# Holding the first token block's instructions to their written order, with the list scheduler ordering the rest

## The chip, the core and the metric

The kernel runs on one core of a Trainium2 chip. The metric is the device time of one execution in microseconds; the time before is 1110.92 us, the median of three runs (1110.46 to 1111.63). A core has five engines that each work through a queue of their own in order: TensorE (PE in the profile, with its weight loads as PEld), VectorE (DVE), ScalarE (ACT), GpSimd (POOL) and SyncE (SP), which issues nearly all DMAs here. They wait for one another through semaphores.

## The reference

An attention layer with two kinds of keys is followed by a mixture of four experts.

```python
k_sum = k.reshape(B, H, nb, block, D).max(axis=3)      # B, H, S, D = 4, 8, 768, 64
v_sum = v.reshape(B, H, nb, block, D).mean(axis=3)     # block 32, so 24 blocks
scores_l = scale * q @ k.T                             # kept only where |i - j| < 16
scores_s = scale * q @ k_sum.T + log(block)
a = softmax(concat([scores_l, scores_s]))
x = (a @ concat([v, v_sum])).reshape(B * S, H * D)     # 3072 tokens x 512
p = domain_probs / domain_probs.sum(-1)
for e in range(4):                                     # w1[e] 512 x 1024, w2[e] 1024 x 512
    out += p[:, e] * (relu(x @ w1[e]) @ w2[e])
```

## The kernel before

Tokens are worked on in eight blocks of 384 (`TB`), two to each batch entry. The attention of a block is cut into eight pieces: four query groups of 96 queries (`QB`) by two groups of four heads (`G`). Piece n is query group n // 2 and head group n % 2; a piece sees a window of 128 keys and the 24 block summaries.

**The first block** (`first_tokens`) is written apart from the rest. Its eight pieces run in the order 0, 2, 4, 6, 1, 3, 5, 7. Every piece has 18 steps: scores in two halves (tile `psc`, 64-row matmuls in f32), maxima and subtraction on DVE (`ms`, `nb`), exponentials on ACT, a summary copy (`sm`), transposes (`pT`), copies out of PSUM (ACT for `pT`, DVE for `sT`), the product with the values (`pav`, called the gather), the division on DVE (`rs`, `xt`), two transposes of the quotient (again into `pav`, called the x turn) and the two parts of the result (`xh` on ACT, `xl` on DVE). Beside the pieces stand block maxima of k (`ksr`, DVE), block means of v by matmul (`pvf`, from `vn`), and, for expert 0, four early halves of the first product (`ph` 0 to 3, the half whose inputs come from head group 0). The table `STEPS` gives each step an offset, `T0` the distance of pieces, `KEYS` the places of the other work; the steps are sorted by these numbers, so the calls are made in an interleaved order that was set by hand.

**All later work** is written in a loop: `plan` names the blocks and experts, and `advance` puts the attention pieces of the next blocks (pieces 8, 9, ... with `stage_a`, `scores`, `probs`, `transposed`, `values`, `to_x`) between the units of the matmuls `ph` (x by w1) and `po` (h by w2). Weights are loaded in raw form (`wr`, four buffers) and split into a high part by ACT and a rest by POOL (w1) or DVE (w2 while one block is worked on). A transposing DMA turns a piece's weights `aw` into `awT`, from which PE makes `px`.

**What sets the order.** No call issues anything: a call appends a `Step` to the list `program`. At the end `order_of(program, bufs_of)` reads the operands, finds which step must follow which (data, and the buffers of each tile tag), and lets a list scheduler with its own costs pick the sequence: each engine takes, among the steps whose inputs are there, the one with the lowest rank, which is PE's nominal time of the work that needs it. The result is issued in that sequence, and that is the order of each engine's queue. So the order in which the first block's calls were made is only one input of the ranks; an engine may take any other ready step first.

`in_order` and `early` do not exist before the change. `Step.behind` maps the number of a step that must come first to a flag: with True the scheduler waits for its end and a semaphore, with False only for its start.

Of the kernel before, what the change touches and what calls it, by code (L numbers as in the profile page):

```python
# [64 lines left out]
WAIT = dict(PE=53, ACT=33, DVE=33, POOL=76, SP=28)  # L65
# [7 lines left out]
@cache  # L73
def footprint(offset, pairs, wide):

    (step, parts), *rest = pairs
    mask = (1 << wide) - 1
    for s, n in reversed(rest):
        if s and n > 1:
            one, mask = mask, 0  # L80
            for k in range(n):
                mask |= one << (s * wide * k)
    return offset // step, offset // step + parts, mask << (offset % step * wide)
# [75 lines left out]
        return 400.0, ((1350.0 if store else 1950.0) + SPARE_DMA, t * 1.2)  # L159


def order_of(steps, bufs):

    used, live = {}, {}
    for n, s in enumerate(steps):
        seen = {}
        for ap, w in [(x, True) for x in s.written] + [(x, False) for x in s.read]:
            name, tag = ap.tensor.name, getattr(ap.tensor, "tag", None)  # L170
            if tag is None:
                continue
            p0, p1, mask = footprint(ap.offset, ap.ap, BYTES[ap.dtype] // 2)
            kept = []
            for at in live.get(name, ()):
                m, a0, a1, was, wrote = at
                if m != n and (w or wrote) and a0 < p1 and p0 < a1:
                    chain = s.key == "PE" == steps[m].key
                    if was & mask or chain:
                        full = not chain and (wrote or steps[m].key != s.key)  # L180
                        s.behind[m] = max(s.behind.get(m, False), full)
                        if w and not was & ~mask and a0 >= p0 and a1 <= p1:
                            continue
                kept.append(at)
            live[name] = [*kept, (n, p0, p1, mask, w)]
            seen[name] = tag
        for name, tag in seen.items():
            used.setdefault(tag, {}).setdefault(name, []).append(n)
        s.tiles = list(seen.items())
        for m, full in s.behind.items():  # L190
            steps[m].ahead.append((n, full))
    queue = {tag: sorted(tiles, key=lambda t: tiles[t][0]) for tag, tiles in used.items()}


    nominal, now = {}, 0.0
    for n, s in enumerate(steps):
        if s.key == "PE":
            nominal[n] = now
            now += s.takes
    freed = {}  # L200
    for tag, names in queue.items():
        for old, new in zip(names, names[bufs[tag] :]):
            first = used[tag][new][0]
            for m in used[tag][old]:
                if m < first:
                    freed.setdefault(m, []).append(first)
    due, place = {}, now
    for n in range(len(steps) - 1, -1, -1):
        s = steps[n]
        place = nominal.get(n, place)  # L210
        end = sum(s.lasts) if s.key == "SP" else s.lasts
        d = [due[m] - (end + WAIT[steps[m].key] if full else s.takes) for m, full in s.ahead]
        d += [due[m] - end - WAIT[steps[m].key] for m in freed.get(n, ())]
        due[n] = min(nominal.get(n, math.inf), *d) if d else nominal.get(n, math.inf)
        if due[n] == math.inf:
            due[n] = place + 30000.0
    rank = [nominal.get(n, due[n]) for n in range(len(steps))]


    left = [len(s.behind) + len(s.tiles) for s in steps]  # L220
    ready = [0.0] * len(steps)
    uses = {name: len(at) for tiles in used.values() for name, at in tiles.items()}
    gone, given = {}, {}
    coming = {k: [] for k in WAIT}
    waiting = {k: [] for k in WAIT}
    free = dict.fromkeys(WAIT, 0.0)
    lanes, wire, order = [0.0] * LANES, 0.0, []

    def loosen(n, t):
        ready[n] = max(ready[n], t)  # L230
        left[n] -= 1
        if not left[n]:
            heapq.heappush(coming[steps[n].key], (ready[n], n))

    def give(tag, t):
        k = given[tag] = given.get(tag, -1) + 1
        if k < len(queue[tag]):
            for n in used[tag][queue[tag][k]]:
                loosen(n, t + WAIT[steps[n].key] if t else 0.0)

    for n, s in enumerate(steps):
        if not left[n]:
            heapq.heappush(coming[s.key], (0.0, n))
    for tag in queue:
        for _ in range(bufs[tag]):
            give(tag, 0.0)
    while len(order) < len(steps):
        best = None
        for k in WAIT:
            t = max(free[k], lanes[0] + WAIT[k]) if k == "SP" else free[k]  # L250
            while coming[k] and coming[k][0][0] <= t:
                n = heapq.heappop(coming[k])[1]
                heapq.heappush(waiting[k], (rank[n], n))
            if not waiting[k]:
                if not coming[k]:
                    continue
                t = coming[k][0][0]
            if best is None or t < best[0]:
                best = t, k
        t, k = best  # L260
        while coming[k] and coming[k][0][0] <= t:
            n = heapq.heappop(coming[k])[1]
            heapq.heappush(waiting[k], (rank[n], n))
        n = heapq.heappop(waiting[k])[1]
        s = steps[n]
        order.append(n)
        free[k] = t + s.takes
        if k == "SP":
            wire = end = max(wire, t + s.lasts[0]) + s.lasts[1]
            lanes = [*lanes[1:], end]  # L270
        else:
            end = t + s.lasts
        for m, full in s.ahead:
            loosen(m, end + WAIT[steps[m].key] if full else t + 1.0)
        for name, tag in s.tiles:
            uses[name] -= 1
            gone[name] = max(gone.get(name, 0.0), end)
            if not uses[name]:
                give(tag, gone[name])
    return order  # L280
# [3 lines left out]
def attn_moe(ctx: ExitStack, tc: tile.TileContext, qvL, qv0, v0L, kD, kT, vT, w1L, w2L, dpL, cst, out):  # L284
    nc = tc.nc
    program, bufs_of = [], {}

    class Engine:
# [11 lines left out]
    V, A, PL, PE, SP = (  # L300
        Engine(e, k)
        for e, k in ((nc.vector, "DVE"), (nc.scalar, "ACT"), (nc.gpsimd, "POOL"), (nc.tensor, "PE"), (nc.sync, "SP"))
    )
# [97 lines left out]
    def mixing():  # L401
        SP.dma_start(pw, dpL)
        s = const.tile([P, NT, 1], F32, name="dps")
        V.tensor_reduce(s, pw, axis=AX.X, op=ALU.add)
        V.tensor_scalar_add(s, s, EPS)
        V.reciprocal(s, s)
        V.tensor_tensor(pw, pw, s.broadcast_to([P, NT, E]), op=ALU.mult)
# [87 lines left out]
    def split_v(b, v0):  # L495
        b12 = sb.tile([NST, 2, 512], BF16, name=f"b12_{b}", tag="awT", bufs=2)
        b1, b2 = b12[:, 0, :], b12[:, 1, :]
        V.tensor_copy(b1, v0)
        V.tensor_tensor(v0, v0, b1, op=ALU.subtract)
        V.tensor_copy(b2, v0)  # L500
        V.tensor_tensor(v0, v0, b2, op=ALU.subtract)
        V.tensor_scalar_mul(b1, b1, gsel[0])
        V.scalar_tensor_tensor(b2, b2, gsel[1], b1, op0=ALU.mult, op1=ALU.add)
        vs = sb.tile([NST, H, D], BF16, name=f"vs{b}", tag="vs", bufs=2)
        V.scalar_tensor_tensor(
            vs,
            v0.rearrange("p (h d) -> p h d", d=D),
            gsel[2],
            b2.rearrange("p (h d) -> p h d", d=D),
            op0=ALU.mult,  # L510
            op1=ALU.add,
        )
        vsum[b] = vs
# [963 lines left out]
    steps = []  # L1477
# [19 lines left out]
    def advance(to):  # L1497
        nonlocal at
        while at < len(steps) and steps[at][0] < to:
            steps[at][1](steps[at][2])  # L1500
            at += 1

    EARLY = 4
    ahead = plain_units([0], 0, early=EARLY)
    first_tokens(ahead)
    mixing()
    advance(per)
    split_v(0, *vmean0)
    V.tensor_tensor(high_rows[:NST], gsel[0], gsel[1], op=ALU.add)


    plan = [([0], (0, 1)), ([1], (1, 0)), ([0, 1], (2, 3)), *PAIRS]
    pos = per
    for (tbs, experts), end in zip(plan, ENDS):
        pair = tbs if isinstance(tbs, int) else None
        n = 2 if pair else len(tbs)
# [25 lines left out]
            part()  # L1542
        pos = end

    for n in order_of(program, bufs_of):
        tc.keep_in_program_order(program[n].issue())


# [59 lines left out]
```

## Time and profile before

| what | value |
|---|---|
| median of three runs | 1110.92 us (1110.46 to 1111.63) |
| profiled execution | 1109.61 us |
| its span | 1107.8 us |
| granted PE clock, mean | 0.979 |
| PE busy | 1093.2 us (99%) |
| DVE, ACT, POOL busy | 806.9, 695.1, 563.8 us |

The profiled execution took 1.31 us less than the median. Its span runs from the first to the last recorded instruction; 1.81 us lie outside it. Line 296 is the line at which the helper `Engine` calls the engine, so every group of the profile stands on that one line, and tiles tell the groups apart. The granted clock is the share of full speed that PE's clock had; "busy" on PE counts a matmul that runs at half clock for its whole doubled length.

### The profile page before, as it was taken

The numbers are of one execution on the slowest core, as the hardware profiler recorded it, in microseconds if no ns is written. First come the engines' busy times: TensorE is split into PE (matmuls) and PEld (weight loads), VectorE is DVE, ScalarE is ACT, GpSimd is POOL, SyncE is SP. The second block draws the span as 40 slices with busy tenths as digits, with TensorE's granted clock in tenths as the row PEclk, the third lists the DMA queues.
The fourth block names the chain that finished last, engine by engine and source line by source line (L and its number), as shares of the span: only waits on it lengthen the run. The fifth ranks groups of instructions, "written<-read, shape, count | busy, mean of one in ns | idle before, by whom it ended". The sixth has DMA issues, their size and how long they took to land.

```text
span 1107.8 us, 20496 instructions
## 1 busy us (share of the span) xinstructions
PE 1093.2 (99%) x6994; PEld 760.3 (69%) x6994; DVE 806.9 (73%) x1959; ACT 695.1 (63%) x1882; POOL 563.8 (51%) x650
## 2 busy tenths in 40 slices
PE   8989999999999999999999999999999999999998
PEld 6888888898898765555555565555555468686867
DVE  4479988998988898878776555556545794969473
ACT  3567867775576999887764565556434581838170
POOL 1378976783764989976643313224112251627050
PEclk8589999999999999999999999999999999999999
DMA  7268757777556698787797564474721350514001
GB/s 269 77 202 232 201 159 186 177 201 188 157 165 193 209 307 244 229 250 228 244 296 213 156 171 133 135 229 123 187 83 38 132 160 14 171 47 162 3 15 58
DMA packets 169305, 184.10 MB, mean 166 GB/s; under 512 B 79344, under 2 KB 115184, under 8 KB 169200
## 3 DMA queue, kind: packets, MB, share of 16 engines
q1 hardware_dynamic: 169200, 182.79, 55.7%
q8 instruction: 55, 0.90, 0.3%
q14 instruction: 50, 0.41, 0.1%
HBM read 131.76 MB, written 34.08 MB: 150 GB/s over the span
## 4 chain that ended last, share of the span: by engine, by line
PE 89%; DVE 3%; POOL 2%; DMA 2%; ACT 2%; issue 1%; SPq 0%; POOLq 0%; ACTq 0%; DVEq 0%
PE po L296 30%; PE phb L296 12%; PE ph L296 11%; PE pha L296 8%; PE psc L296 5%; PE pob L296 4%; PE phc L296 4%; PE phd L296 4%; PE poa L296 3%; PE px L296 2%; PE pav L296 2%; PE pod L296 1%; PE poc L296 1%; DMA wr<-in_w1L 1%; PE pT L296 1%
## 5 line engine op out<-in xcount | busy, mean ns | idle before, releaser
L296 PEld LDWEIGHTS <-w1g 128*128 128x128 f16 x2016 | 195.6, 98 | 145.3 <-issue 2.1
L296 PE MATMUL po<-w2s,h 128*128 128x512 f16 x1152 | 279.8, 379 | 0.0
L296 PEld LDWEIGHTS <-h 128*128 128x128 f16 x1584 | 151.7, 98 | 116.4
L296 PE MATMUL phb<-x_t,w1g 128*128 128x384 f16 x864 | 164.1, 326 | 0.8 <-ACT phb L296 0.3
L296 PE MATMUL ph<-xh,w 128*128 128x384 f32 x512 | 141.1, 346 | 0.4 <-ACT xh L296 0.4
L296 POOL TENSOR_TENSOR ks<-kr,ks 128x304 fp32r<-128x304 f32 x112 | 103.3, 926 | 45.5 <-ACT ks L296 38.2
L296 PE MATMUL po<-w,hh 128*128 128x512 f32 x384 | 123.5, 399 | 0.7 <-DVE hl L296 0.7
L296 ACT ACTIVATE ms<-ms,nb 96x152 f32<-96x152 f32 x256 | 104.5, 414 | 18.0 <-DVE nb L296 17.4
L296 DVE CUSTOM_DVE_ANT_0 ms<-psc,c_sb 96x152 f32<-96x152 f32 x256 | 70.9, 306 | 59.9 <-PE psc L296 57.3
L296 PE MATMUL pha<-x,w1g 128*128 128x384 f16 x576 | 111.5, 326 | 0.0
L296 POOL TENSOR_TENSOR w<-wr,w 128x512 fp32r<-128x512 f32 x60 | 84.0, 1408 | 43.9 <-ACT w L296 38.8
L296 POOL TENSOR_TENSOR qs<-qv,qs 64x384 fp32r<-64x384 f32 x56 | 58.7, 1048 | 91.3 <-ACT qs L296 66.3
L296 PEld LDWEIGHTS ph<-xh,w 128*128 128x128 f32 x512 | 94.8, 192 | 1.3 <-ACT xh L296 0.6
L296 PE MATMUL ph<-xl,w 128*128 128x384 f32 x256 | 87.3, 341 | 0.0
L296 POOL TENSOR_TENSOR v<-qv,v 128x256 f16<-128x256 f32 (+1 forms) x56 | 43.0, 768 | 86.3 <-ACT v L296 78.1
L296 PEld LDWEIGHTS po<-w,hh 128*128 128x128 f32 x384 | 69.7, 188 | 16.0 <-DVE hl L296 1.8
L296 POOL TENSOR_TENSOR w2g<-wr,w2g 128x256 f16<-128x256 f32 (+1 forms) x32 | 31.2, 983 | 90.4 <-ACT w2g L296 90.3
L296 PE MATMUL po<-w,hl 128*128 128x512 f32 x192 | 75.8, 395 | 0.0
L296 DVE TENSOR_TENSOR aw<-ms,aw 96x512 f16<-96x512 f32 x112 | 68.5, 639 | 5.5 <-ACT aw L296 4.7
L296 PE MATMUL psc<-ks,qs 128*96 128x152 f32 x448 | 63.8, 265 | 1.7 <-DVE nb L296 0.9
L296 PEld LDWEIGHTS <-hs 128*128 128x128 f16 x576 | 56.3, 98 | 6.6
L296 PEld LDWEIGHTS psc<-ks,qs 128*96 128x96 f32 x448 | 52.7, 164 | 11.5 <-DVE nb L296 1.4
(184 smaller groups left out, 2250.1 us busy)
## 6 DMA issues: line engine op xcount, KB each, us to landing
wr<-in_w2L SPq DMA_DIRECT2D x104, 256.0 KB, 3.1
qv<-in_qvL SPq DMA_DIRECT2D x56, 320.0 KB, 3.3
kr<-in_kD SPq DMA_DIRECT2D x56, 256.0 KB, 3.5
w1g<-wdg SPq DMA_DIRECT2D x28, 512.0 KB, 3.5
wr<-in_w1L SPq DMA_DIRECT2D x44, 256.0 KB, 3.1
w1g<-wdg SPq DMA_DIRECT2D x28, 384.0 KB, 3.1
wx<-in_w1L SPq DMA_DIRECT2D x32, 256.0 KB, 4.2
wdg<-w1g SPq DMA_DIRECT2D x16, 512.0 KB, 4.2
```

What stands on the lines that cost most here:

```text
L296: program.append(Step(self.key, lambda: getattr(self.engine, name)(*a, **kw), name, a, kw))
```

## The change

`order_of` takes a third argument, `early`, with a step number for each engine. A step whose number lies below its engine's entry is put behind the engine's step before it (flag False). `in_order` is filled twice: with the length of the program after `first_tokens` for all five engines, and again after the mixing weights, `advance(per)` (which puts `stage_a` of piece 8), `split_v` and one small sum, for PE, ACT, DVE and POOL. So SP keeps the written order through `first_tokens`, the other four through `split_v`. Steps written later are free, and may still be taken between two held ones. The arithmetic, the tiles, the buffers and the number of instructions of work stay.

```diff
-def order_of(steps, bufs):
+def order_of(steps, bufs, early):
-    used, live = {}, {}
+    used, live, last = {}, {}, {}
     for n, s in enumerate(steps):
...
         s.tiles = list(seen.items())
+        if n < early[s.key]:
+            if s.key in last:
+                s.behind.setdefault(last[s.key], False)
+            last[s.key] = n
         for m, full in s.behind.items():
             steps[m].ahead.append((n, full))
...
     first_tokens(ahead)
+    in_order = dict.fromkeys(WAIT, len(program))
     mixing()
     advance(per)
     split_v(0, *vmean0)
     V.tensor_tensor(high_rows[:NST], gsel[0], gsel[1], op=ALU.add)
+    in_order.update(dict.fromkeys(("PE", "ACT", "DVE", "POOL"), len(program)))
...
-    for n in order_of(program, bufs_of):
+    for n in order_of(program, bufs_of, in_order):
         tc.keep_in_program_order(program[n].issue())
```

In the rows below the first number in a name is the piece (`psc8`), the block (`ph0`) or the layer and expert of a weight (`w10` is w1 of expert 0), and the last one counts tiles. Line 296 of the kernel before is line 300 of the changed one.

**The start, DVE and SP.** DVE behind the maxima of piece 0, before:

```order
L296 COPY vsf0_124<-c_sb_72 96x4
L296 COPY vsf1_173<-c_sb_72 96x4
L296 TENSOR_TENSOR high_rows_73<-c_sb_72 120x1
L296 TENSOR_TENSOR vsf0_124<-pvf0_120,c_sb_72 96x4x64
L296 ISA ms2_126,nb2_127<-psc2_0_122,c_sb_72 96x152
```

and now:

```order
L300 TENSOR_REDUCE ksr0_91<-k02_79 128x24
L300 TENSOR_TENSOR vsf0_124<-pvf0_120,c_sb_72 96x4x64
L300 COPY vsf0_124<-c_sb_72 96x4
L300 ISA ms2_126,nb2_127<-psc2_0_122,c_sb_72 96x152
L300 ISA nb2_127 96x1
```

The block maxima of the third k chunk, which stood behind the first maxima of piece 4, now stand ahead of the value sums and the maxima of piece 2. SP's ninth to thirteenth transfer, before and now:

```order
L296 DMA qv0_2_83<-in_qv0 128x448
L296 DMA qv0_3_84<-in_qv0 128x448
L296 DMA k02_79<-in_kT 128x768
L296 DMA k03_80<-in_kT 128x768
L296 DMA qv0_4_85<-in_qv0 128x448
```

```order
L300 DMA k02_79<-in_kT 128x768
L300 DMA k03_80<-in_kT 128x768
L300 DMA qv0_2_83<-in_qv0 128x448
L300 DMA qv0_3_84<-in_qv0 128x448
L300 DMA wr10_0_103<-in_w1L 128x512
```

The two k chunks went ahead of the queries of the third and fourth piece, and the first two weight tiles ahead of the last four pieces' queries.

**The end of the first block, PE.** Behind the last scores of piece 7, before:

```order
L296 MATMUL ph0_0_0_215<-xh0_0_96,w10_0_140 128x384
L296 MATMUL ph0_0_0_215<-xl0_0_97,w10_0_140 128x384
L296 MATMUL pav1_188<-c_sb_72,xt1_193 128x96 x2
L296 MATMUL pav3_200<-vsf1_173,sT3_196 96x260
L296 MATMUL pav3_200<-vf3_170,pT3_195 96x65 x4
L296 MATMUL ph0_0_0_215<-xh0_0_96,w10_0_140 128x384 x2
L296 MATMUL ph0_0_0_215<-xl0_0_97,w10_0_140 128x384
L296 MATMUL pT5_202<-c_sb_72,ms5_190 128x96 x4
```

and now:

```order
L300 MATMUL pav3_200<-c_sb_72,xt3_206 128x96 x2
L300 MATMUL pav5_211<-vsf1_173,sT5_209 96x260
L300 MATMUL pav5_211<-vf5_185,pT5_208 96x65 x4
L300 MATMUL pT7_212<-c_sb_72,ms7_203 128x96 x4
L300 MATMUL pT7_212<-c_sb_72,sm7_210 96x96
L300 MATMUL ph0_0_0_215<-xh0_0_96,w10_0_140 128x384
L300 MATMUL ph0_0_0_215<-xl0_0_97,w10_0_140 128x384
L300 MATMUL ph0_0_0_215<-xh0_0_96,w10_0_140 128x384 x2
```

The first matmul of the experts came, before, directly behind the scores of piece 7; now two gathers, two sets of transposes and two x turns stand ahead of it that stood behind it.

**The step onto block 1, PE and SP.** PE around the scores of piece 8, before:

```order
L296 MATMUL psc8_0_244<-ks8_0_232,qs8_234 96x152 x4
L296 MATMUL psc8_1_251<-ks8_1_233,qs8_234 96x152 x4
L296 MATMUL pav7_219<-c_sb_72,xt7_222 128x96 x2
L296 MATMUL ph0_0_0_215<-xh0_1_98,w10_0_140 128x384
L296 MATMUL ph0_0_1_220<-xh0_1_98,w10_1_145 128x384
L296 MATMUL ph0_0_2_224<-xh0_1_98,w10_2_176 128x384
L296 MATMUL ph0_0_3_225<-xh0_1_98,w10_3_201 128x384
L296 MATMUL psc9_0_274<-ks9_0_253,qs9_255 96x152 x4
```

and now, 62 `ph` matmuls behind the x turn of piece 7:

```order
L300 MATMUL ph0_0_6_281<-xh0_0_96,w10_6_280 128x384
L300 MATMUL ph0_0_6_281<-xl0_0_97,w10_6_280 128x384
L300 MATMUL psc8_0_244<-ks8_0_232,qs8_234 96x152 x4
L300 MATMUL psc8_1_251<-ks8_1_233,qs8_234 96x152 x4
L300 MATMUL ph0_0_6_281<-xh0_0_96,w10_6_280 128x384 x2
```

The summaries that piece 8 needs come to their place by four small DMAs, `ks0`. On SP before and now:

```order
L296 DMA wr10_3_106<-in_w1L 128x512
L296 DMA qv8_113<-in_qvL 128x640
L296 DMA kr8_112<-in_kD 128x4x128
L296 DMA ks0_230<-ksr0_91 64x4x24 x4
L296 DMA qv9_115<-in_qvL 128x640
```

```order
L300 DMA qv9_115<-in_qvL 128x640
L300 DMA wr10_4_228<-in_w1L 128x512
L300 DMA wr10_5_229<-in_w1L 128x512
L300 DMA ks0_230<-ksr0_91 64x4x24 x4
L300 DMA wr20_4_265<-in_w2L 128x512
```

They went behind two weight tiles, `wr10_4` and `wr10_5`, whose buffers come free only when DVE has split the w2 tiles 0 and 1, and that split now stands behind the division of piece 5 and of piece 7. The queues of before and now are alike again from the second product of block 1 with expert 1 on (PE's last difference stands there).

## The prediction

> **What bounds the kernel now.** First the page: busy time by engine, the clock row (tenths of full speed in forty slices) and two groups with count, busy and mean ns.
>
> ```profile
> PE 1093.2 (99%) x6994; PEld 760.3 (69%) x6994; DVE 806.9 (73%) x1959; ACT 695.1 (63%) x1882; POOL 563.8 (51%) x650
> PEclk8589999999999999999999999999999999999999
> L296 POOL TENSOR_TENSOR ks<-kr,ks 128x304 fp32r<-128x304 f32 x112 | 103.3, 926 | 45.5 <-ACT ks L296 38.2
> L296 POOL TENSOR_TENSOR w<-wr,w 128x512 fp32r<-128x512 f32 x60 | 84.0, 1408 | 43.9 <-ACT w L296 38.8
> ```
>
> PE is never short of work for long: of 1107.8 us only 14.6 are without a matmul. What can be won is therefore idle time of PE and time at a low clock, and both lie in the first 75 us, the stretch that the change orders anew. The busy time by stretch shows the second (us; busy time and instructions of PE, PEld, DVE, ACT, POOL; granted clock; DMA share; GB/s):
>
> ```profile
> 17.60:55.16 37.56, 37.56 (x193) 32.40 (x193) 17.96 (x81) 18.03 (x53) 9.47 (x12) 0.50 0.34 100
> 55.16:65.40 10.24, 7.78 (x59) 6.77 (x58) 7.96 (x26) 7.19 (x21) 9.62 (x9) 1.00 0.51 165
> 65.40:72.22 6.82, 6.04 (x21) 5.53 (x21) 4.91 (x12) 3.33 (x12) 6.24 (x7) 0.50 0.83 270
> 80.00:100.00 20.00, 19.72 (x125) 16.23 (x124) 18.52 (x44) 15.07 (x45) 16.98 (x18) 1.00 0.74 212
> 100.00:120.00 20.00, 20.00 (x155) 18.60 (x154) 18.98 (x45) 16.79 (x49) 15.55 (x17) 1.00 0.90 243
> 120.00:140.00 20.00, 20.00 (x127) 16.64 (x126) 19.15 (x43) 14.40 (x44) 18.48 (x19) 1.00 0.67 189
> 140.00:160.00 20.00, 20.00 (x132) 18.72 (x131) 17.49 (x50) 12.85 (x38) 14.60 (x16) 1.00 0.55 134
> ```
>
> Half clock holds from 17.60 to 55.16, with PE busy all 37.56 us, and from 65.40 to 72.22, with 6.04 busy. Work at half clock takes twice its time, so (37.56 + 6.04) / 2 = 21.8 us are lost. The first stretch is 11, the full-clock one 3 and the second 2 times 3.413 us: the clock changes on a grid. PE's timeline shows the idle time (start, length, operation, in brackets the idle time before it and what ended it):
>
> ```profile
> 9.05 0.30 PE L296 MATMUL pT<-c_sb,ms 96*128 96x96 f32 x1 [1.55 <-ACT ms L296]
> 9.19 2.78 PE L296 MATMUL pvf<-vn,c_sb 128*120 128x256 f32 x12
> 11.90 0.46 PE L296 MATMUL psc<-k,qv 64*96 64x128 f32 x2
> 13.43 0.47 PE L296 MATMUL pT<-c_sb,ms 96*128 96x96 f32 x3
> 13.91 0.46 PE L296 MATMUL psc<-k,qv 64*96 64x128 f32 x2
> 16.78 0.68 PE L296 MATMUL pav<-vsf,sT 96*96 96x260 f32 x2
> 40.48 0.74 PE L296 MATMUL psc<-k,qv 64*96 64x128 f32 x2
> 42.87 1.18 PE L296 MATMUL pav<-vsf,sT 96*96 96x260 f32 x2
> 49.55 0.69 PE L296 MATMUL ph<-xh,w 128*128 128x384 f32 x1
> 64.39 0.38 PE L296 MATMUL pav<-c_sb,xt 96*128 96x96 f32 x2 [2.05 <-DVE xt L296]
> 65.19 1.49 PE L296 MATMUL ph<-xh,w 128*128 128x384 f32 x4 [0.41 <-ACT xh L296]
> 67.47 0.93 PE L296 MATMUL psc<-ks,qs 128*96 128x152 f32 x4 [0.78 <-POOL qs L296]
> ```
>
> From 11.90 to 13.43 and from 13.91 to 16.78 PE did three half-pieces of scores in 4.40 us; at half clock two took 42.87 - 40.48 = 2.39, so three at full clock are some 1.80. The stall on DVE's maxima is 2.6 us there.
>
> **The change, part by part.** *The start.* PE stands idle for 1.55 + 2.6 = 4.15 us before the clock falls. In the new order the first transposes stand behind the value sums, so the first wait becomes one for `vn`. Those sums ran at 9.19 right behind the transposes, so `vn` was in by then; I take 8.75, a wait of 1.25 (bounds 0 and 1.55). The reduce of the third k chunk now stands ahead of the maxima of piece 2 on DVE:
>
> ```profile
> 17.12 0.94 DVE L296 TENSOR_REDUCE ksr<-k 128x24 f32<-128x768 f32 x1
> 10.77 0.40 POOL L296 COPY vf<-qv 128x256 f32<-128x256 f32 x1 [4.30 <-DMA qv<-in_qv]
> 14.52 0.40 POOL L296 COPY vf<-qv 128x256 f32<-128x256 f32 x1 [2.11 <-DMA qv<-in_qv]
> ```
>
> The chunk moves up two places among transfers that came in between 10.77 and 14.52; I estimate 11.8, so DVE is free of it at 12.7, and PE's next scores wait about 0.55. With 0.35 at the first division the idle time is 2.15: **-2.0**. Bounds: all 4.15 gone, or 1 us lost if the chunk comes at 14.5 and holds DVE.
>
> *The half clock.* What ended it? Of the matmuls `ph` alone, three windows of the grid (same columns, PE and PEld first):
>
> ```profile
> 48.33:51.74 3.41, 1.01 (x2) 0.50 (x2) 0.00 (x0) 0.00 (x0) 0.50 0.01 2
> 51.74:55.16 3.42, 1.93 (x5) 1.55 (x6) 0.00 (x0) 0.00 (x0) 0.50 0.37 91
> 65.40:68.81 3.41, 1.90 (x6) 1.52 (x6) 0.00 (x0) 0.00 (x0) 0.50 0.96 323
> 14.19:17.60 3.41, 2.58 (x22) 2.01 (x21) 1.93 (x10) 2.42 (x7) 0.89 (x4) 1.00 1.05 385
> ```
>
> The clock rose behind the second, where PE was full and 1.93 us were `ph`; not behind the first (1.01), and not behind the third, in which PE also stood idle for 0.78. The last row is of all operations, the window behind which it fell, with PE busy for 2.58 of 3.41. So I take it that the rise needs a full window with about 1.9 us of `ph`. [...]
>
> In the new order two gathers, two sets of transposes and two x turns stand ahead of the first `ph` that stood behind it. Their prices at half clock:
>
> ```profile
> 37.34 1.18 PE L296 MATMUL pav<-vsf,sT 96*96 96x260 f32 x2
> 39.54 0.84 PE L296 MATMUL pT<-c_sb,ms 96*128 96x96 f32 x4
> 50.36 0.52 PE L296 MATMUL pav<-c_sb,xt 96*128 96x96 f32 x2
> 50.67 1.07 PE L296 MATMUL pav<-vsf,sT 96*96 96x260 f32 x2
> ```
>
> A gather goes from 37.34 to 39.54 (2.20), a set of transposes to 40.48 (0.94), an x turn 0.31 (0.40 with its start): 2 x 3.54 = 7.08. PE enters the half clock with 2.0 us of full-clock work done ahead, 4.0 us at half clock. The first `ph` comes at 49.55 + 7.08 - 4.0 = 52.6. From there to 55.16 are 2.5 us of `ph`, enough for the clock to rise at 55.16 as before; had it to wait a window, 58.57, 1.7 us dearer, and two, 3.4. The second stretch of half clock followed the idle time around 62 to 66 and goes with it. What is left is 37.56 / 2 = 18.8: **-3.0** (bounds -3.0 and +0.4).
>
> *The idle time at 62 to 68.* 2.05 + 0.41 + 0.78 us. The last division of piece 7 now has the matmuls of `ph` 0 to 6 behind it, and the scores of piece 8, on which PE waited for POOL, stand behind these: **-3.2** (bounds -3.2 and 0, if the wait only moves).
>
> *New waits.* The weights' splits on POOL now decide when `ph` 4 to 7 run. POOL's written string between weight 4 and weight 7 has three `w` at 1.41, four `ks` at 0.93 by the page's means, two `qs` at about 1.0, two `kr` and smaller ones, some 13.5 us together; by my count PE does seven tiles in that time and comes to `ph` 6 half a us early and to `ph` 7 again: **+1.1** (bounds 0 and 3). Sum at PE: -2.0 - 3.0 - 3.2 + 1.1 = **-7.1**.
>
> *The cap.* PE can be that early only if DVE is. From 80 to 160 DVE is busy 18.52 + 18.98 + 19.15 + 17.49 = 74.1 of 80 us, and each `px` needs DVE's `aw`:
>
> ```profile
> 73.92 0.96 DVE L296 TENSOR_TENSOR aw<-ms,aw 96x512 f16<-96x512 f32 x2
> 93.55 0.40 PE L296 MATMUL px<-awT,v 128*64 128x192 f16 x6 [0.28 <-DMA awT<-aw]
> L296 DVE TENSOR_REDUCE vmax<-vch 128x1 f32<-128x768 f32 x4 | 3.8, 941 | 0.0
> L296 DVE TENSOR_REDUCE wmax<-w 128x1 f32<-128x512 f32 x10 | 6.4, 666 | 0.0
> L296 DVE SCALAR_TENSOR_TENSOR hl<-ph,hh 128x384 fp32r<-128x384 f32 x20 | 10.9, 547 | 3.5 <-ACT hh L296 3.3
> L296 DVE SCALAR_TENSOR_TENSOR xs<-px,xs 128x192 f32<-128x192 f32 x8 | 2.7, 343 | 0.9 <-ACT xs L296 0.9
> ```
>
> (The group rows are DVE's between 60 and 160 us.) By my count of the held string, DVE does the `aw` of piece 8 around 79.0 instead of 74.9, with 2.95 us of later work already done: 1.15 behind. But ahead of the `aw` of piece 15 four reductions of `vch`, two `wmax`, one `hl` and one `xs` drop out: 4 x 0.94 + 2 x 0.67 + 0.55 + 0.34 = 6.0. DVE's lead there is 6.0 - 1.15 = 4.8, and about as much where the queues become alike again. So of PE's 7.1 about **5.0** stay: 1109.6 - 5.0 = 1104.6 for an execution like the profiled one. That one lies 1.3 below the median, so the forecast is **1105.9**.
>
> **The rivals.** *One episode, no gain.* PE catches up with the attention at the `px` of piece 8: the `ks0` DMAs, which carry the block summaries, now stand on SP behind two weight tiles that wait for DVE's split of the w2 tiles, so the scores and the `aw` are late. A second stall of the kind at 62 to 68 would cost 3.2 us and two windows of half clock, 3.0: 6.3. -5.0 + 6.3 gives 1112.2; a DVE that gives nothing of the gain on gives 1110.4. For it speaks the small slack at 93.55 (PE waits there for `awT` by 0.28 already); against it that POOL, not `ks0`, ended PE's wait at 67.47.
>
> *Slower: two episodes.* If `ks0` comes so late that pieces 8 and 9 both hold PE, each stall ends in half clock: -5.0 + 12.6 = 1118.5. It decides once `awT` lands 2.4 us or more behind PE's coming to `px`, since a wait of 2.05 and its sequel were what went before the fall at 65.40. Against it: `ph` and `po` of expert 0 lie between, and `ks0` needs only two splits of 0.9 us of DVE's.
>
> *The clock never falls.* [...] As a mechanism here: the fall at 17.60 followed a window of 2.58 busy, and the new order fills that window. It would give 18.8 more at PE, as far as DVE and the transfers let it: 1105.9 - 18.8 = 1087. Against it, at 0.50 full windows did not help; and the rows do not tell what made it fall.
>
> *The hold does nothing* is out: PE's queue differs in a thousand places.
>
> **How the numbers follow.** Within 0.2% (2.2 us) a measurement of this kernel cannot be told from no change. The forecast with its spread (first half clock up to two windows longer, the cap a few us off) has a chance of 0.63, its own range 1102 to 1108.7; the clock that never falls 0.05; one episode or nothing 0.19; two episodes 0.13. The range of 1101.5 to 1111 leaves out the clock's rival, the slower one and the tail of the third. Faster is 0.63 + 0.05 = 0.68, the same 0.19, slower 0.13.
>
> **What would show it.** Right: idle time of PE before 17.6 near 2 us; half clock once, to 55.16; no half clock at 65 to 72; no wait of PE for `xt` of piece 7; waits below 1 us for the POOL tiles of `ph` 6 and 7; DVE some 5 us earlier at 160. Wrong: `px` of piece 8 waiting for `awT` by us and a half clock behind it; a first `ph` behind 53.2, with the clock up at 58.57 or 61.98; or 1.00 in all windows.

## The result and the profile after

The changed kernel takes 1098.70 us (median of four, 1096.94 to 1100.42) against 1110.69 us for the kernel before (median of four): a ratio of 0.9893, 95% interval 0.9874 to 0.9912. That is 12 us less; 5.0 had been forecast, and the time lies below the range. The profiled execution took 1096.94 us with a span of 1095.2. All ratios here leave out executions more than 1.5% above the fastest of the same kernel.

Its page, busy time by engine and the clock in forty slices:

```profile
PE 1077.9 (98%) x6994; PEld 747.4 (68%) x6994; DVE 810.6 (74%) x1959; ACT 694.9 (63%) x1882; POOL 563.9 (51%) x650
PEclk9999999999999999999999999999999999999999
```

The dip of the first two slices, from the half clock between 17.60 and 55.16 us, is gone. PE is busy for 15.3 us less with the same 6994 matmuls, and idle for 17.3 us instead of 14.6. So the span's 12.6 us are 15.3 us of less time at half clock, less 2.7 us of new waits. The windows of the clock's grid, of PE alone (length, PE busy and instructions, granted clock, DMA share, GB/s), before:

```profile
7.36:10.77 3.41, 1.86 (x12) 1.00 1.05 404
10.77:14.19 3.42, 3.01 (x20) 1.00 1.04 399
14.19:17.60 3.41, 2.58 (x22) 1.00 1.05 385
17.60:21.01 3.41, 3.41 (x24) 0.50 1.01 352
```

and after:

```profile
7.85:11.27 3.42, 2.55 (x12) 1.00 1.04 407
11.27:14.68 3.41, 3.41 (x33) 1.00 1.06 394
14.68:18.09 3.41, 3.41 (x34) 1.00 1.04 386
18.09:21.51 3.42, 3.42 (x32) 1.00 1.00 321
52.23:55.64 3.41, 1.95 (x14) 1.00 0.74 225
55.64:59.05 3.41, 3.41 (x14) 0.50 0.32 87
```

The window behind which the clock fell is now full, and the clock stays up through all eight pieces, until PE waits at 53 us. PE's timeline shows its first wait, for the values `vn`; in two gathers one piece apart how long a piece takes at full clock; and in the first `ph` the lead that PE wins (49.55 before):

```profile
8.72 2.82 PE L300 MATMUL pvf<-vn,c_sb 128*120 128x256 f32 x12 [0.98 <-DMA vn<-in_v0L]
18.05 0.68 PE L300 MATMUL pav<-vsf,sT 96*96 96x260 f32 x2
21.81 0.68 PE L300 MATMUL pav<-vsf,sT 96*96 96x260 f32 x2
37.67 0.42 PE L300 MATMUL ph<-xh,w 128*128 128x384 f32 x1
53.16 0.91 PE L300 MATMUL psc<-ks,qs 128*96 128x152 f32 x8 [0.81 <-POOL qs L300]
54.72 0.62 PE L300 MATMUL ph<-xh,w 128*128 128x384 f32 x2 [0.65 <-POOL w L300]
93.87 0.44 PE L300 MATMUL ph<-xh,w 128*128 128x384 f32 x1 [1.31 <-ACT w L300]
151.55 0.92 PE L300 MATMUL psc<-ks,qs 128*96 128x152 f32 x4 [3.30 <-DVE nb L300]
```

A piece takes 21.81 - 18.05 = 3.76 us. PE leads by 11.9 us at the first `ph`. A landmark that exists once, the transpose `pmx` behind the maxima of v (tile view: count, times, first and last start), shows it again later, before and after:

```profile
L296 PE MATMUL pmx<-c_sb,vm x1: 276/276/276, 140.7 to 140.7; 128*1 128x128 f32 x1
L300 PE MATMUL pmx<-c_sb,vm x1: 276/276/276, 124.9 to 124.9; 128*1 128x128 f32 x1
```

The lead is 15.8 us there and 12.6 at the end. The wait of 3.30 us at 151.55 takes most of the difference; half clock follows it (0.91 on the mean from 140 to 160):

```profile
80.00:100.00 20.00, 16.84 (x122) 15.02 (x121) 19.21 (x44) 16.99 (x53) 19.45 (x23) 1.00 0.86 220
140.00:160.00 20.00, 16.70 (x92) 14.38 (x90) 17.94 (x44) 12.94 (x35) 12.80 (x14) 0.91 0.58 172
```

(columns as in the prediction's first windows). From 80 to 100 PE is idle for 3.16 us. Its waits name the splits of the weights, 1.31 and 1.13 us for ACT's part and 0.72 for POOL's. DVE and POOL, busy for 19.21 and 19.45 of 20 us, are likely the bound behind them; no run tests that.

### The profile page after: what moved, and what is told of

Same layout as the page of the kernel before. It is cut to its first block, busy times and chain, and to the rows that moved or that the text cites. A ratio compares the mean times of both kernels' runs of the same rounds, so it can differ in the third digit from the quotient of the medians.

```text
span 1095.2 us, 20517 instructions
## 1 busy us (share of the span) xinstructions
PE 1077.9 (98%) x6994; PEld 747.4 (68%) x6994; DVE 810.6 (74%) x1959; ACT 694.9 (63%) x1882; POOL 563.9 (51%) x650
## 4 chain that ended last, share of the span: by engine, by line
PE 86%; DVE 5%; POOL 3%; ACT 3%; issue 1%; DMA 1%; SPq 0%; POOLq 0%; DVEq 0%; ACTq 0%
PE po L300 30%; PE phb L300 12%; PE ph L300 9%; PE pha L300 8%; PE psc L300 4%; PE pob L300 4%; PE phc L300 4%; PE phd L300 4%; PE poa L300 3%; PE px L300 2%; PE pod L300 1%; PE poc L300 1%; PE pav L300 1%; DVE wmax L300 1%; DVE ms L300 1%
## 5 line engine op out<-in xcount | busy, mean ns | idle before, releaser
L300 DVE TENSOR_TENSOR aw<-ms,aw 96x512 f16<-96x512 f32 x112 | 73.3, 681 | 8.2 <-ACT aw L300 7.8
```

Source lines behind the costliest of these rows:

```text
L300: program.append(Step(self.key, lambda: getattr(self.engine, name)(*a, **kw), name, a, kw))
```

## The experiments

Theory A, formed from these windows: the gain is the clock. Idle time of PE among the small f32 matmuls of the pieces lets it fall, and at half clock these matmuls never raise it again, however full PE is. Theory B: the fall has another cause (the order, the mix of matmuls), or the order brings the gain by itself. Each kernel is compared with the kernel before on the same chip (medians 1109.9 to 1111.5); two changed kernels are compared by their ratios. In experiments 2, 8, 9 and 11 the executions of one kernel lie up to 24 us apart, which is the finding there.

### 1. A stall put back

The changed kernel, with four reduces ahead of the maxima of piece 6.

```diff
...
+    junk = const.tile([P, NB], F32, name="junk")
+    first = min(n for n, s in enumerate(program) if s.written[0].tensor.name.rpartition("_")[0] == "ms6")
     for n in order_of(program, bufs_of, in_order):
+        for _ in range(4 * (n == first)):
+            x = kch0[0].rearrange("p (n b) -> p n b", b=BLK)
+            tc.keep_in_program_order(nc.vector.tensor_reduce(junk, x, axis=AX.X, op=ALU.max))
         tc.keep_in_program_order(program[n].issue())
```

(`kch0` holds the tiles of the k chunks; nothing reads `junk`.)

> The changed kernel with four extra reduces on VectorE (0.94 us each, 3.8 us together, results unused) ahead of the maxima of piece 6, near 17 us; nothing else moves. Theory A (a stall of PE lets the granted clock fall, and the small f32 matmuls of the pieces then never raise it): PE stands idle for 2.5 to 3.8 us near 17 us, the clock is at 0.50 from about 18 to 21 us until the first matmuls ph, which come near 58 instead of 37.7, and the time is 1108 to 1118, about that of the kernel before. Theory B (what made the clock fall in the kernel before is not idle time but its order or mix of matmuls): the clock stays at 1.00 to 50 us and the time is that of the change plus at most the stall, 1098.7 to 1102.5.

Measured: 1117.42 us (eight executions, 1113.81 to 1120.06), ratio to before 1.0051 (1.0032 to 1.0071), 18.7 us above the change. Its windows of PE, then three rows of its timeline:

```profile
20.07:23.49 3.42, 3.15 (x30) 1.00 0.55 116
23.49:26.90 3.41, 0.63 (x5) 1.00 0.47 182
26.90:30.31 3.41, 3.41 (x20) 0.50 0.00 0
54.21:57.62 3.41, 3.41 (x18) 0.50 0.66 218
57.62:61.03 3.41, 3.41 (x26) 1.00 0.28 76
```

```profile
26.27 0.38 PE L300 MATMUL pav<-c_sb,xt 96*128 96x96 f32 x2 [3.04 <-DVE xt L300]
42.10 1.18 PE L300 MATMUL pav<-vsf,sT 96*96 96x260 f32 x2
48.98 1.18 PE L300 MATMUL pav<-vsf,sT 96*96 96x260 f32 x2
```

One wait of 3.04 us, and the clock is at 0.50 for nine full windows, until `ph` runs. Theory A holds, B's time (at most 1102.5) is missed by 15 us. Between the last two gathers lie 6.88 us: a piece at half clock takes 6.88 / 3.76 = 1.83 times its time, not twice.

### 2 and 5. The order of before, with the idle time filled

Eight and then sixteen extra matmuls on PE; the queues are otherwise those of the kernel before, row by row.

```diff
...
+    extra = {last[tile]: k for tile, k in {'psc2_0': 2, 'pT0': 2, 'psc2_1': 2, 'psc4_0': 2}.items()}
+    z, pz = warm
     for n in order_of(program, bufs_of):
         tc.keep_in_program_order(program[n].issue())
+        for _ in range(extra.get(n, 0)):
+            tc.keep_in_program_order(nc.tensor.matmul(pz, z[:, 0:P], z, start=True, stop=True))
```

(`last` holds the number of the last PE step that writes a tile; `z` and `pz` are the operand and the target of the matmuls with which the kernel starts anyway. In experiment 5 the counts are three for each of these four tiles, and two each for `psc4_1` and `psc6_0`.)

> The kernel before with eight extra 128x512 bf16 matmuls (about 0.37 us each, results unused) on PE, two each behind the scores psc2_0, the transposes pT0, and the scores psc2_1 and psc4_0, where PE stands idle between 12 and 17 us; the order of all the rest is that of before. Theory A: the clock stays at 1.00 past 17.6 us, the first ph comes near 38 to 40 instead of 49.55, and the time falls by 8 to 12 us to 1099 to 1103 (the stalls at 62 to 68 and DVE take some of it). Theory B: half clock from about 17.6 to 55 us as before, and 1110 to 1112.

> The kernel before with sixteen extra 128x512 bf16 matmuls instead of eight (three each behind psc2_0, pT0, psc2_1 and psc4_0, two each behind psc4_1 and psc6_0; results unused), everything else in the order of before. With eight the time went with the clock that each execution had: 1096.8 at a mean clock of 0.995, 1101.4 at 0.989, 1110.9 at 0.980. If the whole gain of the change is the clock, most executions now keep 1.00 to 50 us and take 1097 to 1103, no slower than the change, though the order is that of before. If the order brings a gain of its own, they stay 4 us or more above the change's 1098.7 even at a clock of 0.99 and above.

Measured with eight: 1096.79 to 1115.02 us in ten executions, median 1109.27. The time goes with the mean clock of the execution:

| mean clock | us |
|---|---|
| 0.995 and 0.994 | 1096.79, 1097.78 |
| 0.989 | 1101.39, 1101.48 |
| 0.985 | 1107.62 |
| 0.980 | 1110.93 |
| 0.978 and 0.977 | 1113.04, 1113.39, 1114.17, 1115.02 |

About 1 us for each thousandth. The expectation that eight would do in every execution was wrong. With sixteen: 1097.34 us (1097.03 to 1099.82, clock 0.994 to 0.997), ratio 0.9875 (0.9855 to 0.9894). The order of before, with its clock up, is no slower than the changed order (1098.70, and the ratios' intervals overlap), though it carries sixteen matmuls more. So within the some 2 us that these intervals leave, the change gains by the clock alone. Two windows of PE in experiment 5, near the place of the old fall and with extra matmuls in them, keep full clock; the old wait for `xt` of piece 7 is still there, earlier by 11 us:

```profile
15.03:18.44 3.41, 3.00 (x20) 1.00 1.05 384
18.44:21.85 3.41, 3.00 (x23) 1.00 0.79 267
```

```profile
53.32 0.39 PE L296 MATMUL pav<-c_sb,xt 96*128 96x96 f32 x2 [2.05 <-DVE xt L296]
```

One window of this execution, from 8.20 to 11.61, did stand at half clock, against the expectation; the next was at full clock again.

### 3. The hold ends with the first block

```diff
-    in_order.update(dict.fromkeys(("PE", "ACT", "DVE", "POOL"), len(program)))
```

> The hold ends with the first token block for all five engines; the mixing weights, the preparation of piece 8 and the split of v are free. Theory A: the gain is made before 50 us and by the clock, so 1.00 to 50 us and 1097 to 1101. Rival C (the late part of the hold, which puts the scores of piece 8 behind the matmuls ph, brings a good part of it): stalls of PE at the scores of piece 8 come back and with them a stretch of half clock, 1102 to 1106.

Measured: 1098.76 us (1097.02 to 1100.21), ratio 0.9883 (0.9853 to 0.9913), as fast as the change; rival C falls. But not for theory A's reason alone: the clock was at 0.989 to 0.992. Its windows of PE, its DVE and its PE timeline:

```profile
22.89:26.31 3.42, 3.42 (x31) 1.00 0.00 0
26.31:29.72 3.41, 2.71 (x26) 1.00 0.23 75
29.72:33.13 3.41, 3.41 (x18) 0.50 0.03 7
```

```profile
26.93 1.25 DVE L300 TENSOR_TENSOR v<-v,b 120x512 f32<-120x512 f32 x1
28.10 0.41 DVE L300 TENSOR_TENSOR xt<-pav,rs 96x256 f32<-96x256 f32 x1
```

```profile
28.56 0.38 PE L300 MATMUL pav<-c_sb,xt 96*128 96x96 f32 x2 [0.70 <-DVE xt L300]
```

A product of the v split, now free, slipped in ahead of a division; PE waited 0.70 us, and 17 us of half clock followed. That the time is the change's all the same means that the free tail wins about what the fall costs; experiment 7 tries this.

### 4. SP free

```diff
+    in_order["SP"] = 0
```

> SP is free, the other four engines are held as in the change. The scheduler then puts one k chunk and the block summaries ks0 earlier. Theory A with the start on DVE and PE alone: no stall over 1 us before 20 us, the clock at 1.00 to 50 us, 1097 to 1101; and with ks0 earlier, PE waits less than 1.5 us for POOL between 52 and 56 us. Rival D (SP's order is what fills PE before 17.6 us): idle time of PE over 2 us before 18 us, half clock from then to about 55 us, 1105 to 1112.

Measured: 1095.53 us (1094.11 to 1098.59, clock 0.995 to 0.998), ratio 0.9858 (0.9826 to 0.9890). The median is 3.2 us below the change's, but the two intervals overlap, so a gain over the change isn't shown. Rival D falls by its time, but not by its mechanism. With SP free two waits for DVE's maxima are back, where the changed kernel has PE full from 11.27 to 52.23 us:

```profile
14.35 0.34 PE L300 MATMUL psc<-ksr,qv 64*96 64x24 f32 x2 [0.45 <-DVE nb L300]
16.44 0.26 PE L300 MATMUL psc<-ksr,qv 64*96 64x24 f32 x1 [0.41 <-DVE nb L300]
```

So SP's order is part of what fills PE; why the waits return wasn't traced. The clock stood at half from 8.61 to 12.02 in the profiled execution, against the expectation, and then held in spite of the waits. Experiment 8, with the same first transfers, shows that this isn't safe.

### 6. Heavy matmuls in the midst of the half clock

The kernel before, with fourteen extra 128x512 matmuls behind `pvf1`, put in as in experiment 2.

```diff
+    extra = {last[tile]: k for tile, k in {'pvf1': 14}.items()}
```

> The kernel before with fourteen extra 128x512 bf16 matmuls on PE in one row behind the repeats pvf1, near 35 us, in the midst of the stretch of half clock in which PE is fully busy anyway (results unused). Theory A (what counts is the work done in a window of 3.41 us, and the small matmuls at half clock do too little): the clock rises within two windows of the first of them, by 43 us, and stays at 1.00 through the rest of the pieces; the extra matmuls cost about 8 us of PE and the earlier rise gives about 7 back, so 1109 to 1114. Theory A2 (only the share of busy time counts, and something else kept the clock low): PE is as busy as before, the clock stays at 0.50 until ph, and the time is 1116 to 1121.

Measured: 1106.64 us (1104.83 to 1109.70), ratio 0.9964 (0.9946 to 0.9981), some 2 us below the range of theory A. Windows of PE and the row of the extra matmuls:

```profile
31.89:35.31 3.42, 3.42 (x20) 0.50 0.01 2
35.31:38.72 3.41, 3.41 (x12) 0.50 0.56 166
38.72:42.13 3.41, 3.41 (x20) 1.00 0.00 0
```

```profile
36.63 4.22 PE L1555 MATMUL pz<-z 128*128 128x512 bf16 x14
```

PE is full in all three windows; only the one that holds two us of large matmuls is followed by full clock, at 38.7 instead of 55.2 us, and it stays through the rest of the pieces. Busy time alone doesn't raise the clock here; which matmuls fill it matters. Matmuls of no use made the kernel faster.

### 7, 8 and 9. A version that beats both

Experiment 7 drops the late hold and lets DVE's steps written behind the first block start only behind the division of piece 7; 8 frees SP as well; 9 adds eight extra matmuls to 8, two each behind `psc2_0`, `psc2_1`, `psc4_0` and `psc4_1`.

```diff
-    in_order.update(dict.fromkeys(("PE", "ACT", "DVE", "POOL"), len(program)))
+    gate = max(n for n, s in enumerate(program) if s.written[0].tensor.name.rpartition("_")[0] == "xt7")
+    for s in program[in_order["DVE"] :]:
+        if s.key == "DVE":
+            s.behind[gate] = False
```

> The hold ends with the first token block, as in the kernel with pieces only, but VectorE's steps of the mixing weights, the preparation of piece 8 and the split of v may start only behind the division of piece 7. In the kernel with pieces only a product of the v split (1.25 us) stood ahead of a division and PE waited 0.70 us, whereupon the clock fell from 29.7 to 46.8. Theory A: without that guest the clock stays at 1.00 to 50 us, and the time falls below that kernel's 1098.8 by up to 8 us: 1092 to 1097. Rival: the 8.5 us of half clock were hidden behind VectorE's later work, and the time stays at 1097 to 1100.

> As the kernel before it in this list, with SP free as well. SP free brought 3 us with the late hold (1095.5 against 1098.7), by the block summaries and piece 8 coming earlier. If the two add up: 1090 to 1095. If the limit is VectorE between 60 and 150 us, where it is busy 96 to 98%, no better than 1094 to 1097.

> The kernel with VectorE's later steps kept behind the division of piece 7 and SP free, with eight extra 128x512 bf16 matmuls (results unused), two each behind psc2_0, psc2_1, psc4_0 and psc4_1. Without them its executions fell into two groups, 1091 to 1093 where the clock stayed up (0.997) and 1111 to 1114 where it fell near 17 us (0.975 to 0.978). Theory A: PE has idle time of 2 x 0.41 us and more before 18 us, the clock falls or not by how it lies in the windows, and the extra matmuls fill it: all executions at 0.994 or more and 1091 to 1096. Rival: two groups again.

Measured for 7: 1093.90 us (1092.91 to 1095.16, clock 0.996 to 0.998), ratio 0.9836 (0.9816 to 0.9856): the best that is steady, 4.8 us below the change. For 8: 1091.14, 1092.24 and 1093.27 us at 0.997 to 0.998, but 1110.96 to 1113.81 at 0.975 to 0.978 in the other seven. For 9 (ratio 0.9853, 0.9810 to 0.9895): 1091.71, 1093.07 and 1097.35 us, and once 1116.19 at 0.975, against the expectation; three of four against three of ten are too few to say that the extra matmuls help. The fall of experiment 8, in PE's windows:

```profile
9.85:13.27 3.42, 2.90 (x19) 1.00 1.04 398
13.27:16.68 3.41, 3.00 (x28) 1.00 1.04 389
16.68:20.09 3.41, 3.41 (x21) 0.50 0.99 357
```

A window with 0.41 us without a matmul was enough here. Experiment 7 differs by SP's order alone; its PE is full from 10.51 to 51.47 us, and all four executions kept their clock. Three of the ten executions of 8 kept theirs; that the waits lay otherwise in their windows would explain it, but only the profiled execution shows windows. The kernel of experiment 4 passed such a window:

```profile
15.43:18.85 3.42, 3.01 (x30) 1.00 1.05 382
```

### 10 and 11. PE alone, DVE alone

```diff
+    in_order = {k: n if k == "PE" else 0 for k, n in in_order.items()}
```

(with `"DVE"` in experiment 11)

> Only PE is held (through the split of v); SP, VectorE, ScalarE and GpSimd are free. If PE's own order (value sums ahead of the first transposes) is what keeps it busy before 18 us: less than 0.5 us idle between 11 and 18 us, clock at 1.00 to 50 us, 1093 to 1100. If VectorE's or SP's order is needed: waits of PE of 0.4 us and more for the maxima, a fall near 17 us in some or all executions, 1109 to 1114 there.

> Only VectorE is held (through the split of v). If VectorE's order alone keeps PE busy before 18 us, the clock stays at 1.00 and the time is 1093 to 1101; if PE's own order is needed, the fall near 17 us is there and the time is 1107 to 1114.

Measured with PE alone held: 1111.02 us (eight executions, 1109.23 to 1114.33), ratio 1.0005 (0.9989 to 1.0021), the whole gain gone. Its PE waits for the maxima as before, and the clock falls at 17.2 us:

```profile
15.12 0.34 PE L300 MATMUL psc<-ksr,qv 64*96 64x24 f32 x2 [0.41 <-DVE nb L300]
17.21 0.35 PE L300 MATMUL psc<-ksr,qv 64*96 64x24 f32 x1 [0.41 <-DVE nb L300]
```

With DVE alone held: one execution of 1098.36 and one of 1119.38 us, at a mean clock of 1.000 and 0.974. The 1.000 can't be trusted: two scores `psc` took 0.74 us at 9.91 and 0.46 at 18.04, as in the kernel before at 0.50 (0.74 at 40.48) and at 1.00 (0.46 at 11.90), so PE ran at half clock at first. Two executions decide little; they only show that DVE's order by itself doesn't secure the clock either.

### 12. The wait at 150 us

The kernel of experiment 7, with the maxima of the weights ranked later.

```diff
+    for n, s in enumerate(steps):
+        if s.written[0].tensor.name.rpartition("_")[0] in ("wmax", "wmax_0") or s.written[0].tensor.name.startswith("wmax"):
+            rank[n] += 6000.0
```

> The kernel with VectorE's later steps behind the division of piece 7 (median 1093.9), in which the scheduler's ranks of all maxima of the weights (wmax) are set 6 us later. There, 13 of them in a row (7.8 us) held VectorE from 141.3 to 149.0, PE waited 1.61 us for the maxima of a piece, and half clock followed from 150.5 to 153.9 (1.7 us lost). Now seven of the 13 stand behind those maxima. If such a stall costs its idle time and the window of half clock behind it at the end too: 1.6 + 1.7 us less, 1090 to 1092. If what PE gains there is lost again at the next wait for VectorE: 1093 to 1095.

Measured: 1095.52 us (1094.17 to 1097.26), ratio 0.9856 (0.9833 to 0.9879): no better than experiment 7. The wait and its half clock are gone, but from 200 to 300 us PE is now idle for 2.19 us, where it was 0.22; it waits there for DVE, 1.5 us for a part of a weight and 0.7 for `hl`. (The profiled execution also had two windows of half clock before 20 us, which experiment 7's had not; but the executions at a clock of 0.998, 1094.17 and 1094.73 here and 1092.91 and 1093.52 there, say the same.) The rows of experiment 7 and of this one:

```profile
140.00:160.00 20.00, 18.39 (x100) 15.42 (x99) 16.72 (x49) 13.97 (x39) 12.70 (x14) 0.91 0.56 169
200.00:300.00 100.00, 99.78 (x622) 87.95 (x621) 88.98 (x237) 64.86 (x186) 67.45 (x68) 1.00 0.70 192
```

```profile
140.00:160.00 20.00, 20.00 (x127) 17.18 (x126) 18.12 (x49) 14.06 (x38) 11.67 (x12) 1.00 0.67 184
200.00:300.00 100.00, 97.81 (x611) 85.70 (x611) 89.95 (x228) 64.02 (x186) 68.72 (x69) 1.00 0.69 185
```

## Why the prediction was wrong

**The start** was right in its mechanism, and its number in part by luck. By the windows PE was idle for 2.79 us between 7.36 and 17.60 before, and for 0.87 between 7.85 and 18.09 now: -1.9 where -2.0 stood. The terms came out otherwise. The wait for `vn` was 0.98 (1.25 forecast), and the two waits of 0.55 and 0.35 didn't come. And the 2.6 of the stall on the maxima were too many: the scores that took 4.40 us take 0.89 and 1.37 in the changed kernel (11.47 to 12.36 and 12.92 to 14.29), not 1.80, which leaves 2.1. By that measure, which counts what the windows take for busy, 3.7 us became 1.0.

**The half clock** is the step that failed, and it carries the error: -3.0 stood there, with half clock kept from 17.60 to 55.16. It never came, because what had brought it was the very idle time that the first step had just taken away. The prediction had the row for it, 2.58 of 3.41 us busy in the window behind which the clock fell, and gave this course 0.05, since "at 0.50 full windows did not help". Those windows tell of the rise and say nothing of the fall. In the runs, the windows of pieces behind which the clock fell held idle time of PE: 0.41 us of 3.41 (experiment 8), 0.70 (experiment 3) and 0.83 (the kernel before). Full windows of these small matmuls didn't raise it (ten before, 17.60 to 51.73, and five in experiment 6, 18.24 to 35.31).

**The price of half clock** was mis-sized in the same step. "Twice its time", and the "doubled length" ahead of the prediction, were estimates from the granted clock of 0.50, and no run shows them: a piece takes 1.83 times as long, and a `ph` takes 0.52 us instead of 0.33, with 0.32 from one start to the next instead of 0.17 (the kernel before, two rows at 0.50 and two at 1.00):

```profile
69.56 0.52 PE L296 MATMUL ph<-xh,w 128*128 128x384 f32 x1
69.88 0.52 PE L296 MATMUL ph<-xl,w 128*128 128x384 f32 x1
72.52 0.33 PE L296 MATMUL ph<-xh,w 128*128 128x384 f32 x1
72.69 0.33 PE L296 MATMUL ph<-xl,w 128*128 128x384 f32 x1
```

43.6 us of PE's busy time lay at half clock before and 6.5 lie there now (two windows); 37.1 x (1 - 1/1.83) = 16.8, against 15.3 by which PE's busy time fell. The difference isn't accounted for further. The rival had the mechanism, and its 1087 was too low: the stretch that it priced at 18.8 is worth 17.0 at 1.83, and PE is now idle for 6.5 us from 80 to 100 and 140 to 160 together, where it was 0.3.

**The idle time at 62 to 68** went as forecast for `xt` and `xh` (2.46 us). PE's wait for POOL at the scores of piece 8 only moved: 0.78 before, 0.81 at 53.16.

**The new waits** for POOL's splits came to 0.65 at 54.72, where 1.1 stood. What wasn't seen is that this wait and the one that moved leave 1.46 us of one window without a matmul and cost a window of half clock besides, 55.64 to 59.05, by estimate some 1.5 us (3.41 x (1 - 1/1.83)).

**The cap** of 5.0 was wrong. It had DVE do the `aw` of piece 8 around 79.0, a date that rested on pieces at half clock. It came much sooner:

```profile
61.26 1.29 DVE L300 TENSOR_TENSOR aw<-ms,aw 96x512 f16<-96x512 f32 x2
```

It starts at 61.3 instead of 73.9, and PE's lead at `pmx` is 15.8 us. That DVE limits PE further on is right: the 3.30 us at 151.55 are a wait for DVE's maxima, by which the lead shrinks to 12.8 at the next landmark (the first `pmw`, 165.1 and 152.3), and experiment 12 shows a gain in this stretch lost again at a later wait for DVE.

**The slower rivals** did not come. What SP's order, with `ks0` behind the weight tiles, costs isn't shown (experiment 4's intervals overlap the change's); PE's waits from 50 to 200 us name `awT` nowhere.

**What stays open.** What exactly is counted in a window isn't known. Windows of the pieces alone let the clock fall at 2.58, 2.71 and 3.00 us busy and kept it at 3.01 and 3.15; windows with large matmuls kept it at 2.02 (the changed kernel, from 93.19) and lost it at 2.23 (experiment 1, from 71.27) and 2.62 (experiment 2, from 14.53), so busy time isn't the measure there either. What makes the pieces' matmuls too little to raise the clock, their rows, their columns or the transposes among them, wasn't varied by itself. Nor was it tried, beyond SP, PE alone and DVE alone, which engines must be held together.

## What to carry to other kernels

Look for the window ahead of each fall of the granted clock. Here 0.41 us without a matmul in a window of small ones went before half clock from 16.68 to 61.05 us (experiment 8, whose executions took 1111 to 1114 us with a mean clock of 0.975 to 0.978 and 1091 to 1093 with 0.997 to 0.998), and 0.70 us before half clock from 29.72 to 46.79 (experiment 3); in both the clock rose only behind the first `ph` (58.92 and 44.57). Price an order by the gaps that it leaves in such stretches, not by their sum: sixteen matmuls of no use there (1097.34 us, experiment 5), or other work kept off the engine on which PE waits (1093.90, experiment 7), did here no less than the new order (1098.70). And when an early step of a sum removes idle time, work out the later steps, the clock above all, with that time gone.

## What the runs showed of the hardware

- The pieces' matmuls (f32, 24 to 260 columns), with PE full, kept full clock for as long as no gap came (seven windows from 11.27 to 35.16 us in the changed kernel) and didn't raise half clock in ten full windows (17.60 to 51.73 before; 1.01 us of the last were `ph`). Large ones raised it within a window of 3.41 us: bf16 with 512 columns in experiment 6, and the value sums `pvf`, f32 with 128 rows and 256 columns, in experiment 4 (3.38 us busy from 8.61 to 12.02 at 0.50, then 1.00).
- At half clock (0.50) a piece took 1.83 times as long (6.88 us in experiment 1 against 3.76 in the changed kernel).
- The grid lay otherwise in three profiled executions (the falls at 17.60 in the kernel before, 17.94 in experiment 2 and 16.68 in experiment 8 are no whole windows of 3.41 us apart). That would explain how one and the same kernel, with such gaps, takes 1091 or 1113 us (experiment 8); it isn't shown, since each kernel has one profile.
